# Packed attention and a gated product on one core: the gate of 96 units by Softplus and Erf in groups of three instead of a chain of tanh

## The chip, the core and the metric

The kernel runs on one core of a Trainium2 chip. Five engines work side by side, each through its own instructions in order: TensorE (PE in the profile; its weight loads are PEld), VectorE (DVE), ScalarE (ACT), GpSimd (POOL) and SyncE (SP, which issues most DMAs). The metric is the device time of one execution in microseconds.

## The reference, cut to what matters

```
scale = 1.0 / np.sqrt(q.shape[-1])               # q, k, v: 8 x 8 x 576 x 64, p: 8 x 8 x 32 x 64
p_packed = sm_attn(p, k, v)                      # softmax(scale * p k^T) v: 32 rows per head
out = sm_attn(q, p_packed, p_packed)             # softmax over those 32
x = out.transpose(0, 2, 1, 3).reshape(B * S, H * D)   # 4608 x 512
h = x @ w_in                                     # 4608 x 2048
sp = np.maximum(h, 0.0) + np.log1p(np.exp(-np.abs(h)))
g = h * erf(sp)
y = g @ w_out                                    # 4608 x 512
```

What is changed is how `h * erf(softplus(h))` is computed, and the order of the work around it.

## The kernel before, in words

The second softmax and `w_in` are joined: for each of the 8 batches b the kernel multiplies the packed rows into `w_in` (`w_prime`, tiles wp, wph and wpl), so that h is wp times the softmax weights a2. The work on h is cut into 128 **units**: batch b, half c of its 576 rows (288 columns) and pair i of 128-blocks of the 2048 features. Unit n of the batches from 2 on is n = 32 + 16 (b - 2) + 8 c + i; units 0 to 31 belong to batches 0 and 1. For every unit:

- `h_half` twice: 6 matmuls each into one of the two banks of the pool `ps_h`, with a2 and wp cut into a high and a low part (float32r for batches 0 and 1, float16 from unit 32 on);
- `h_copy` twice: ACT copies a bank into the tile hs; only then can the bank be written again. The score products of the attention (L386, L507) and a few wp take banks of the same pool, in turn with h;
- the gate. Units 0 to 31: `softplus` (ACT, tile t), `erf` (ACT, in place) and `gate` (DVE, t times hs into hs). The two functions are in different tables of ACT, so the units go in groups of three: `ENDS` lists the unit that closes each group, and after its Softplus come an ACT_TABLE_LOAD, three Erf and three gates. Units 32 to 127: `tanh_gate`, four passes of ACT (L669, L671, L672, L676) and three of DVE (L673, L674, L678), all in the table that has the exponential of the attention, so that no load is needed;
- `split`: DVE makes gh, hs rounded (a cast), and gl, what is left;
- `o_part` for each of four 128-blocks d of the output: 6 matmuls of gh and gl with `w_out`'s two parts, summed over the 4 or 8 units of a segment in one bank of `ps_o` for each d. After a segment's last unit `put` lets ACT copy each bank (tile ob), and a DMA writes it out.

Units 0 to 19 are written out by hand in `BEGINNING`, a letter and numbers for each part. From unit 20 on `step(n, ...)` issues for unit n `h_half` and `h_copy`, then the output product of a unit some way behind: five behind up to unit 31, then two units per step until it is `LAG` = 3 behind. The attention of the next batch is a generator; `ATTEND` and `ATTEND_LATER` say at which step and in which place each piece runs. A pair (n, w) is step n (in `ATTEND_LATER` counted from the first unit of the batch before), and w is the place: 5 behind h, 0 and 1 behind the first `o_part`, 3 behind the third, 2 at the end of the step. `JOINS_LATER` does it for wp: in the steps -6, -4, 2 and 4 from a batch's first unit, wp stands behind the first `o_part`, and its copies wph (ACT, L560) and wpl (DVE) at the end. `keep_order` makes PE, DVE and ACT keep the order in which the code issues.

Two exponentials are of interest: that of the first softmax (tile a, L453, two passes and a sum each, behind the maximum m; then the transposes t, L403, read it), and that of the second (tile ta, L297, one pass).

Of the kernel before, what the change touches and what calls it, by code (L numbers as in the profile page):

```python
# [8 lines left out]
F32 = mybir.dt.float32  # L9
# [11 lines left out]
T_SCALE, T_BIAS = 0.2627170245906788, -0.9287499984171923  # L21
Q_SCALE, Q_BIAS = 1.2484601345862187, 1.2510285994602417
U_SCALE, U_BIAS = 2.981034033350855, 0.5025259929887246
A1, A2 = -1.0780370417831138, 7.315330971479113
A_SCALE, A_BIAS = 0.5000167827005251, 0.3105391086974029
# [17 lines left out]
o10.2 o11.2 v12 s15 L13 h16.0 p11.2 p11.0 h16.1 c16.1 K14 m13 R14 o12.2 d16.0 s16 K13 S13 u13 v13 p11.3 e14 T13  # L43
# [7 lines left out]
def tile_pack_attention_moe(ctx: ExitStack, tc: tile.TileContext, qT, kT, v, pT, w_in, w_out, outT):  # L51
# [17 lines left out]
    LAG = 3  # L69
# [7 lines left out]
    ENDS = (1, 4, 7, 10, 13, 16, 19, 22, 25, 28, 31)  # L77
    BEGUN, BEHIND = 20, 15
# [12 lines left out]
    consts = cpool.tile([P, 2], F32, name="consts")  # L91
# [13 lines left out]
    for i, c in enumerate((8.0 * T_SCALE, 8.0)):  # L105
        nc.gpsimd.memset(consts[:, i:i + 1], c)
# [101 lines left out]
    def scales(b):  # L208

        rho[b] = apool.tile([P, 1], F32, name=f"rho{b}", tag="rho")  # L210
        nc.vector.tensor_scalar(rho[b][:], inverse[b][:], inverse["in"][:], 2.0 ** 11, op0=ALU.mult, op1=ALU.mult)
        back = apool.tile([P, 1], F32, name=f"back{b}", tag="back")
        other_way(back[:], rho[b][:])
        gate_scales[b] = apool.tile([P, 2], F32, name=f"gs{b}", tag="gs")
        nc.vector.tensor_scalar(gate_scales[b][:], consts[:], back[:], None, op0=ALU.mult)
        inverse[b] = back
# [38 lines left out]
    def in_turn(ins):  # L255

        if functions:
# [16 lines left out]
    ATTEND_LATER = ((-12, 2), (-6, 0), (-6, 1), (-4, 0), (-4, 1), (-4, 2), (-3, 2), (-2, 3), (-2, 2), (-1, 3), (-1, 2),  # L274
                    (0, 0), (0, 1), (1, 0), (1, 1), (2, 0), (2, 1), (4, 0), (4, 1),
                    (5, 2), (6, 2), (7, 2), (7, 2), (8, 2), (8, 2), (9, 2), (10, 2), (10, 2))
# [43 lines left out]
    def attention(b):  # L320
# [206 lines left out]
        every = second_softmax(b, ta, tb, mx, hi, lo, 0, S, None, nc.vector.tensor_copy if b < NB0 else nc.scalar.copy)  # L527
# [43 lines left out]
    def h_half(n, k):  # L571
        b, c, i = units[n][:3]
        if k == 0:
            turn = sum(n > e for e in ENDS) % 2
            tag = TAGS[n] if n < ALONE else "t1" if n < GROUPED and turn else "hs"
            rows[n] = tpool.tile([P, 2, HT], F32, name=f"hs{b}_{c}_{i}", tag=tag)
# [16 lines left out]
    def h_copy(n, k, copy=nc.scalar.copy):  # L593
        dst, src = rows[n][:, k, :], banks_of.pop((n, k))[:, 0:HT]
        if n < GROUPED:
            copy(dst, src)
        else:
            nc.scalar.mul(dst, src, 2.0 ** -19)  # L598

    def softplus(n):  # L600
        b, c, i = units[n][:3]
        ts[n] = tpool.tile([P, 2, HT], F32, name=f"t{b}_{c}_{i}", tag="t0")
        in_turn(nc.scalar.activation(ts[n][:], rows[n][:], AF.Softplus))
# [57 lines left out]
    def tanh_gate(n):  # L661

        b, c, i = units[n][:3]
        hs = rows.pop(n)
        t = tpool.tile([P, 2, HT], F32, name=f"t{b}_{c}_{i}", tag="t0")
        u = tpool.tile([P, 2, HT], F32, name=f"u{b}_{c}_{i}", tag="t1")
        scale = gate_scales[b]
        root = A2 ** 0.5
        nc.scalar.activation(t[:], hs[:], AF.Tanh, bias=T_BIAS, scale=scale[:, 0:1])  # L669
        yield  # L670
        nc.scalar.activation(t[:], t[:], AF.Square, bias=root * Q_BIAS, scale=root * Q_SCALE)  # L671
        nc.scalar.activation(u[:], t[:], AF.Tanh, bias=U_BIAS, scale=U_SCALE / A2)  # L672
        nc.vector.scalar_tensor_tensor(t[:], hs[:], scale[:, 1:2], t[:], op0=ALU.mult, op1=ALU.add)  # L673
        nc.vector.scalar_tensor_tensor(t[:], u[:], A1, t[:], op0=ALU.mult, op1=ALU.add)  # L674
        yield
        nc.scalar.activation(t[:], t[:], AF.Tanh, bias=A_BIAS, scale=A_SCALE)  # L676
        yield
        nc.vector.scalar_tensor_tensor(hs[:], t[:], 1.0, hs[:], op0=ALU.add, op1=ALU.mult)  # L678
        gs[n] = (hs,)
        yield  # L680
        yield

    gates, group = {}, []
# [5 lines left out]
    def step(n, outs):  # L689

        now, before = None, gates.pop(n - 1, None)
        late = n == GROUPED
        more = len(outs) > 1
        last = n >= len(units) - 1

        def begin():
            nonlocal now
            if n >= GROUPED:
                now = gates[n] = tanh_gate(n)
            else:  # L700
                group.append(n)

        def functions():
            if now:
                next(now)
            if last:
                split_behind(outs[0])
            if now:
                next(now)
            elif n < GROUPED:  # L710
                softplus(n)

        def split_behind(m):
            if m + 2 < len(units):
                split(m + 2)

        if n < len(units):
            h_half(n, 0)
            if not late:
                h_copy(n, 0)  # L720
            h_half(n, 1)
            if not late:
                h_copy(n, 1)
                do(n, 5)
                begin()
        if before:
            next(before)
            next(before)
        for m in outs:
            for d in range(NDM):  # L730
                o_part(m, d)
                if units[m][4]:
                    put(m, d)
                if m == outs[0] and d == 0:
                    do(n, 0)
                    do(n, 1)
                    if not more:
                        functions()
                        if GROUPED <= n and not last:
                            split_behind(m)  # L740
                elif m == outs[0] and d == 2:
                    do(n, 3)
            if more or n < GROUPED:
                split_behind(m)
        if n in ENDS:
            for part in (erf, gate):
                for m in group:
                    part(m)
            group.clear()
        if late:  # L750
            nc.scalar.preload_act_table_set("exp_and_others")
            do(n, 4)
            for k in range(2):
                h_copy(n, k)
            begin()
        if more:
            functions()
# [29 lines left out]
    for b in range(NB0, B):  # L787
        base = first_use[b - 1]
        for n, where in ATTEND.get(b) or [(base + n, where) for n, where in ATTEND_LATER]:
# [15 lines left out]
    for i, high, low in ((0, 28, 29), (1, 28, 30), (2, 29, 30), (3, 30, 31), (4, 31, 32), (5, 32, 33), (6, 32, 35), (7, 34, 37)):  # L805
        slot(22 + i // 2, 1).append((whole, i))
        slot(high, {6: 4, 7: 5}.get(i, 0)).append((halve_high, i))
# [51 lines left out]
    split(BEHIND + 1)  # L859
    behind = BEHIND  # L860
    for n in range(BEGUN, len(units) + LAG):
        outs = range(behind, min(behind + 1 + (n >= GROUPED), n - LAG + 1))
        step(n, outs)
        behind += len(outs)
# [39 lines left out]
```

## Time and profile before

| | |
|---|---|
| time, median of 3 runs | 693.34 us (693.13 to 693.34) |
| time of the profiled execution | 693.22 us |
| its span in the profile | 691.4 us |
| busy: PE, DVE, ACT | 678.2, 600.3, 556.0 us |
| idle of ACT before L676 / of DVE before L673 | 40.6 / 50.5 us |

The span is from the first to the last instruction that the profile holds; the time has some 1.8 us more around it. A matmul's row lasts from its issue to its modelled end, and the next one's begins before it ends, so PE can be shown as busy while its issue has a short pause. The chain of work that ended last books each matmul from the end of the one before.

### The profile page before, as it was taken

To read this page: it belongs to the slowest core of one execution; us is meant where nothing else is said; L and a number is where in the kernel's file an instruction comes from. 1 tells how busy PE (TensorE), PEld (TensorE's weight loads), DVE (VectorE), ACT (ScalarE), POOL (GpSimd) and SP (SyncE) were. 2 spreads that over 40 slices of the span, in tenths; PEclk is the share of its full clock that TensorE was granted. 3 is DMA by queue.
4 is the path that set the end of the run, shared out by engine and by line. 5 is a ranking of instruction groups with operands and counts; after the bars stand their busy time and mean duration, and the time that the engine had idled before them with its cause. 6 is when DMAs were issued, how large, how long until landed. Compare 5 with 4: busy or idle time off the path is not lost.

```text
span 691.4 us, 15628 instructions
## 1 busy us (share of the span) xinstructions
PE 678.2 (98%) x6442; PEld 537.8 (78%) x6442; DVE 600.3 (87%) x937; ACT 556.0 (80%) x981; POOL 53.6 (8%) x80
## 2 busy tenths in 40 slices
PE   8899999999999999999999999999999999999997
PEld 6687989998889777867777776777777677777775
DVE  4999998989997999889978898888988899877775
ACT  3799977967778789888888888887888878787774
POOL 2031123101452000000000000000000000000000
PEclk9999999999999999999999999999999999999999
DMA  9996456367342502211122202031021101000010
GB/s 317 401 341 217 155 171 228 105 207 230 40 91 22 163 11 86 87 59 42 36 61 95 92 1 73 18 122 66 9 82 52 37 1 36 1 9 27 5 33 34
DMA packets 34311, 66.81 MB, mean 97 GB/s; under 512 B 4032, under 2 KB 13248, under 8 KB 34240
## 3 DMA queue, kind: packets, MB, share of 16 engines
q1 hardware_dynamic: 29600, 56.31, 24.1%
q0 software_dynamic: 4352, 8.92, 5.3%
q8 instruction: 50, 0.82, 0.5%
q10 hardware_dynamic: 288, 0.59, 0.2%
q14 instruction: 21, 0.17, 0.1%
HBM read 49.81 MB, written 15.99 MB: 95 GB/s over the span
## 4 chain that ended last, share of the span: by engine, by line
PE 60%; DVE 18%; ACT 14%; DMA 4%; issue 3%; POOL 0%; SPq 0%; ACTq 0%; POOLq 0%; DVEq 0%
PE o L640 35%; PE h L588 18%; DVE t L673 3%; DVE t L674 3%; PE wp L541 3%; ACT t L671 3%; ACT t L669 2%; DVE gl L623 2%; ACT u L672 2%; ACT t L676 2%; DMA wi<-w_in 2%; ACT ob L652 2%; PE p L415 1%; DMA k<-kT 1%; PE s L507 1%
## 5 line engine op out<-in xcount | busy, mean ns | idle before, releaser
L640 PE MATMUL o<-gh,woh 128*128 128x288 f16 x1536 | 304.3, 286 | 0.9 <-ACT ob L652 0.9
L640 PEld LDWEIGHTS <-woh 128*128 128x128 f16 x2304 | 223.4, 98 | 67.3 <-issue 11.7
L640 PE MATMUL o<-gl,woh 128*128 128x288 f16 x768 | 219.6, 286 | 0.5 <-DVE gl L623 0.4
L588 PE MATMUL h<-a2h,wph 128*128 128x288 f16 (+1 forms) x512 | 148.8, 291 | 1.9 <-ACT hs L598 0.9
L588 PE MATMUL h<-a2h,wpl 128*128 128x288 f16 (+1 forms) x512 | 147.8, 289 | 1.2 <-DVE wpl L565 1.2
L588 PE MATMUL h<-a2l,wph 128*128 128x288 f16 (+1 forms) x512 | 147.5, 288 | 0.0
L673 DVE SCALAR_TENSOR_TENSOR t<-hs,gs,t 128x576 f32<-128x576 f32 x96 | 78.3, 816 | 50.5 <-ACT u L672 49.8
L623 DVE TENSOR_TENSOR gl<-hs,gh 128x576 f16<-128x576 f32 (+1 forms) x124 | 96.3, 776 | 4.4 <-ACT gh L616 0.5
L640 PE MATMUL o<-gh,wohl 128*128 128x288 f32 x448 | 97.9, 299 | 0.8 <-ACT ob L650 0.8
L676 ACT ACTIVATE t<-t 128x576 f32<-128x576 f32 x96 | 65.8, 686 | 40.6 <-DVE t L674 38.8
L598 ACT ACTIVATE hs<-h 128x288 f32<-128x288 f32 x192 | 71.8, 407 | 30.5 <-PE h L588 28.5
L588 PEld LDWEIGHTS <-wph 128*128 128x128 f16 x768 | 74.9, 98 | 20.8 <-issue 1.9
L640 PEld LDWEIGHTS o<-gh,wohl 128*128 128x128 f32 x448 | 74.2, 188 | 7.2 <-issue 2.7
L674 DVE SCALAR_TENSOR_TENSOR t<-u,t 128x576 f32<-128x576 f32 x96 | 72.7, 758 | 3.3
L678 DVE SCALAR_TENSOR_TENSOR hs<-t,hs 128x576 f32<-128x576 f32 x96 | 72.0, 750 | 2.4 <-ACT t L676 2.4
L669 ACT ACTIVATE t<-hs,gs 128x576 f32<-128x576 f32 x96 | 73.8, 769 | 0.0
L671 ACT ACTIVATE t<-t 128x576 f32<-128x576 f32 x96 | 65.6, 683 | 3.0
L672 ACT ACTIVATE u<-t 128x576 f32<-128x576 f32 x96 | 65.6, 683 | 3.1
L640 PE MATMUL o<-gl,wohl 128*128 128x288 f32 x224 | 66.2, 296 | 0.1
L616 DVE CAST gh<-hs 128x576 f16<-128x576 f32 (+1 forms) x117 | 55.6, 475 | 4.1 <-PE o L640 3.7
L588 PEld LDWEIGHTS <-wpl 128*128 128x128 f16 x384 | 37.6, 98 | 9.5
L640 PEld LDWEIGHTS o<-gl,wohl 128*128 128x128 f32 x224 | 42.2, 188 | 0.3 <-DVE gl L623 0.3
(126 smaller groups left out, 823.6 us busy)
## 6 DMA issues: line engine op xcount, KB each, us to landing
q<-qT SPq DMA_DIRECT2D x32, 288.0 KB, 4.1
k<-kT SPq DMA_DIRECT2D x30, 288.0 KB, 4.9
wos<-w_out SPq DMA_DIRECT2D x16, 512.0 KB, 5.7
outT<-ob SPq DMA_DIRECT2D x48, 144.0 KB, 1.8
v<-v SPq DMA_DIRECT2D x24, 256.0 KB, 4.1
wi<-w_in SPq DMA_DIRECT2D x12, 512.0 KB, 6.6
outT<-ob POOLq DMA_DIRECT2D x32, 144.0 KB, 3.3
scratch<-wo POOLq DMA_DIRECT2D x16, 256.0 KB, 3.3
```

The source lines that it names most:

```text
L588: nc.tensor.matmul(ps[:, 0:HT], w[:, r, fo:fo + P], a[:, r, c * HT:(c + 1) * HT], start=(m == 0), stop=(m == 5))
L598: nc.scalar.mul(dst, src, 2.0 ** -19)
L616: copy(ghi[:], gs[n][0][:])
L623: nc.vector.tensor_tensor(glo[:], hs[:], ghi[:], op=ALU.subtract)
L640: nc.tensor.matmul(acc[b, c, d][:, 0:HT], w[f][:, d * P:(d + 1) * P], gg[:, k, :], start=(first and k == 0 and m == 0), stop=(last and k = ...
L669: nc.scalar.activation(t[:], hs[:], AF.Tanh, bias=T_BIAS, scale=scale[:, 0:1])
L671: nc.scalar.activation(t[:], t[:], AF.Square, bias=root * Q_BIAS, scale=root * Q_SCALE)
L672: nc.scalar.activation(u[:], t[:], AF.Tanh, bias=U_BIAS, scale=U_SCALE / A2)
L673: nc.vector.scalar_tensor_tensor(t[:], hs[:], scale[:, 1:2], t[:], op0=ALU.mult, op1=ALU.add)
L674: nc.vector.scalar_tensor_tensor(t[:], u[:], A1, t[:], op0=ALU.mult, op1=ALU.add)
L676: nc.scalar.activation(t[:], t[:], AF.Tanh, bias=A_BIAS, scale=A_SCALE)
L678: nc.vector.scalar_tensor_tensor(hs[:], t[:], 1.0, hs[:], op0=ALU.add, op1=ALU.mult)
```

## The change

From unit 32 on the gate is what it was for units 0 to 31: Softplus (with the batch's scale as a per-partition operand), Erf and one product, in groups of three (`ENDS` now runs to unit 127; groups close at units 1, 4, 7, ...). `tanh_gate`, its constants and its three DVE passes are gone, and so is the step in which the output product caught up: `LAG` is 5 to the end. DVE, not ACT, casts a2. The attention's pieces stand elsewhere: the two exponentials of every batch from 3 on stand at the end of a step that closes a group, behind its three Erf, which needs three versions of `ATTEND_LATER`, since the batches' first units fall on different places in a group. In `BEGINNING` L13 (ACT, part of a weight load) stands behind two `put`, and K13 and S13 (DVE) behind a split.

```diff
-o10.2 o11.2 v12 s15 L13 h16.0 p11.2 p11.0 h16.1 c16.1 K14 m13 R14 o12.2 d16.0 s16 K13 S13 u13 v13 p11.3 e14 T13
+o10.2 o11.2 v12 s15 h16.0 p11.2 p11.0 h16.1 c16.1 L13 K14 m13 R14 o12.2 d16.0 s16 u13 v13 K13 S13 p11.3 e14 T13
...
-    LAG = 3
+    LAG = 5
...
-    ENDS = (1, 4, 7, 10, 13, 16, 19, 22, 25, 28, 31)
-    BEGUN, BEHIND = 20, 15
+    ENDS = tuple(range(1, 16 * B, 3))
+    BEGUN = 20
...
-        gate_scales[b] = apool.tile([P, 2], F32, name=f"gs{b}", tag="gs")
-        nc.vector.tensor_scalar(gate_scales[b][:], consts[:], back[:], None, op0=ALU.mult)
+        gate_scales[b] = apool.tile([P, 1], F32, name=f"gs{b}", tag="gs")
+        nc.vector.tensor_scalar(gate_scales[b][:], back[:], 4.0, None, op0=ALU.mult)
...
-        3: ((25, 2), (27, 0), (27, 1), (30, 0), (30, 1), (31, 2), (32, 2), (34, 3), (34, 2), (35, 3), (35, 2),
+        3: ((25, 2), (27, 0), (27, 1), (30, 0), (30, 1), (31, 1), (31, 2), (34, 3), (34, 2), (35, 3), (35, 2),
...
-    ATTEND_LATER = ((-12, 2), (-6, 0), (-6, 1), (-4, 0), (-4, 1), (-4, 2), (-3, 2), (-2, 3), (-2, 2), (-1, 3), (-1, 2),
-                    (0, 0), (0, 1), (1, 0), (1, 1), (2, 0), (2, 1), (4, 0), (4, 1),
-                    (5, 2), (6, 2), (7, 2), (7, 2), (8, 2), (8, 2), (9, 2), (10, 2), (10, 2))
+    SCORES = ((-12, 2), (-6, 0), (-6, 1), (-4, 0), (-4, 1))
+    POOLED = ((-2, 3), (-2, 2), (-1, 3), (-1, 2), (0, 0), (0, 1))
+    PACKED = ((1, 0), (1, 1), (2, 0), (2, 1), (4, 0), (4, 1))
+    ATTEND_LATER = (
+        SCORES + ((-4, 2), (-2, 2), (-1, 3), (-1, 2), (0, 0), (0, 1), (0, 3), (0, 2)) + PACKED
+        + ((5, 2), (6, 2), (7, 2), (8, 3), (8, 2), (8, 2), (9, 2), (10, 2), (10, 2)),
+        SCORES + ((-4, 2), (-3, 2)) + POOLED + PACKED
+        + ((5, 2), (6, 3), (6, 2), (7, 2), (8, 2), (8, 2), (9, 2), (10, 2), (10, 2)),
+        SCORES + ((-4, 3), (-4, 2)) + POOLED + PACKED
+        + ((5, 2), (6, 2), (8, 2), (9, 3), (9, 2), (9, 2), (10, 2), (11, 2), (11, 2)))
...
-        every = second_softmax(b, ta, tb, mx, hi, lo, 0, S, None, nc.vector.tensor_copy if b < NB0 else nc.scalar.copy)
+        every = second_softmax(b, ta, tb, mx, hi, lo, 0, S, None, nc.vector.tensor_copy)
...
-            tag = TAGS[n] if n < ALONE else "t1" if n < GROUPED and turn else "hs"
+            tag = TAGS[n] if n < ALONE else "t1" if turn else "hs"
...
-            nc.scalar.mul(dst, src, 2.0 ** -19)
+            nc.scalar.mul(dst, src, 2.0 ** -18)
...
     def softplus(n):
         b, c, i = units[n][:3]
         ts[n] = tpool.tile([P, 2, HT], F32, name=f"t{b}_{c}_{i}", tag="t0")
-        in_turn(nc.scalar.activation(ts[n][:], rows[n][:], AF.Softplus))
+        scale = 1.0 if n < GROUPED else gate_scales[b][:, 0:1]
+        in_turn(nc.scalar.activation(ts[n][:], rows[n][:], AF.Softplus, scale=scale))
...
-    def tanh_gate(n):
-        b, c, i = units[n][:3]
-        hs = rows.pop(n)
-        t = tpool.tile([P, 2, HT], F32, name=f"t{b}_{c}_{i}", tag="t0")
-        u = tpool.tile([P, 2, HT], F32, name=f"u{b}_{c}_{i}", tag="t1")
-        scale = gate_scales[b]
-        root = A2 ** 0.5
-        nc.scalar.activation(t[:], hs[:], AF.Tanh, bias=T_BIAS, scale=scale[:, 0:1])
-        yield
-        nc.scalar.activation(t[:], t[:], AF.Square, bias=root * Q_BIAS, scale=root * Q_SCALE)
-        nc.scalar.activation(u[:], t[:], AF.Tanh, bias=U_BIAS, scale=U_SCALE / A2)
-        nc.vector.scalar_tensor_tensor(t[:], hs[:], scale[:, 1:2], t[:], op0=ALU.mult, op1=ALU.add)
-        nc.vector.scalar_tensor_tensor(t[:], u[:], A1, t[:], op0=ALU.mult, op1=ALU.add)
-        yield
-        nc.scalar.activation(t[:], t[:], AF.Tanh, bias=A_BIAS, scale=A_SCALE)
-        yield
-        nc.vector.scalar_tensor_tensor(hs[:], t[:], 1.0, hs[:], op0=ALU.add, op1=ALU.mult)
...
-    def step(n, outs):
-        now, before = None, gates.pop(n - 1, None)
-        late = n == GROUPED
-        more = len(outs) > 1
-        last = n >= len(units) - 1
-        def begin():
-            nonlocal now
-            if n >= GROUPED:
-                now = gates[n] = tanh_gate(n)
-            else:
-                group.append(n)
-        def functions():
-            if now:
-                next(now)
-            if last:
-                split_behind(outs[0])
-            if now:
-                next(now)
-            elif n < GROUPED:
-                softplus(n)
-        def split_behind(m):
-            if m + 2 < len(units):
-                split(m + 2)
+    def step(n, m):
         if n < len(units):
-            h_half(n, 0)
-            if not late:
-                h_copy(n, 0)
-            h_half(n, 1)
-            if not late:
-                h_copy(n, 1)
-                do(n, 5)
-                begin()
-        if before:
-            next(before)
-            next(before)
-        for m in outs:
-            for d in range(NDM):
-                o_part(m, d)
-                if units[m][4]:
-                    put(m, d)
-                if m == outs[0] and d == 0:
-                    do(n, 0)
-                    do(n, 1)
-                    if not more:
-                        functions()
-                        if GROUPED <= n and not last:
-                            split_behind(m)
-                elif m == outs[0] and d == 2:
-                    do(n, 3)
-            if more or n < GROUPED:
-                split_behind(m)
+            for k in range(2):
+                h_half(n, k)
+                h_copy(n, k)
+            do(n, 5)
+            group.append(n)
+        for d in range(NDM):
+            o_part(m, d)
+            if units[m][4]:
+                put(m, d)
+            if d == 0:
+                do(n, 0)
+                do(n, 1)
+                if n < len(units):
+                    softplus(n)
+            elif d == 2:
+                do(n, 3)
+        if m + 2 < len(units):
+            split(m + 2)
         if n in ENDS:
             for part in (erf, gate):
-                for m in group:
-                    part(m)
+                for x in group:
+                    part(x)
             group.clear()
-        if late:
-            nc.scalar.preload_act_table_set("exp_and_others")
-            do(n, 4)
-            for k in range(2):
-                h_copy(n, k)
-            begin()
-        if more:
-            functions()
         do(n, 2)
...
-        slot(high, {6: 4, 7: 5}.get(i, 0)).append((halve_high, i))
+        slot(high, 0 if i < 6 else 5).append((halve_high, i))
...
-    split(BEHIND + 1)
-    behind = BEHIND
+    split(BEGUN - LAG + 1)
     for n in range(BEGUN, len(units) + LAG):
-        outs = range(behind, min(behind + 1 + (n >= GROUPED), n - LAG + 1))
-        step(n, outs)
-        behind += len(outs)
```

Counted over the whole program, ACT has 103 ACT_TABLE_LOAD where it had 30, and 833 rows where it had 958; DVE has 742 where it had 928; PE has the same 8421.

On ACT, in the step of unit 76 (batch 4, c 1, i 4: hs4_1_4 is its h, a1_6 the scores of batch 6, wph5_1 a part of wp of batch 5), before:

```order
L598 ACTIVATE hs4_1_4_5813<-h4_1_4_0_5814 128x288
L598 ACTIVATE hs4_1_4_5813<-h4_1_4_1_5822 128x288
L676 ACTIVATE t4_1_3_5781<-t4_1_3_5781 128x576
L350 COPY a1_6_5690<-s1_1_6_0_5847 128x288
L350 COPY a1_6_5690<-s1_1_6_1_5848 128x288
L669 ACTIVATE t4_1_4_5859<-hs4_1_4_5813,gs4_4583 128x576
L671 ACTIVATE t4_1_4_5859<-t4_1_4_5859 128x576
L672 ACTIVATE u4_1_4_5860<-t4_1_4_5859 128x576
L560 ACTIVATE wph5_1_5888<-wp5_1_5838,rho5_5703 128x1024
L598 ACTIVATE hs4_1_5_5907<-h4_1_5_0_5908 128x288
L598 ACTIVATE hs4_1_5_5907<-h4_1_5_1_5916 128x288
```

The same place in the changed kernel, from this unit's Softplus (L603) to the first h copy of unit 77:

```order
L603 ACTIVATE t4_1_4_5562<-hs4_1_4_5515,gs4_4386 128x576
L652 ACTIVATE ob4_0_7_1_5570<-o4_0_0_1_5148,omega4_4388 128x288
L652 ACTIVATE ob4_0_7_2_5579<-o4_0_0_2_5155,omega4_4388 128x288
L652 ACTIVATE ob4_0_7_3_5603<-o4_0_0_3_5162,omega4_4388 128x288
L606 ACT_TABLE_LOAD
L606 ACTIVATE t4_1_2_5438<-t4_1_2_5438 128x576
L606 ACTIVATE t4_1_3_5491<-t4_1_3_5491 128x576
L606 ACTIVATE t4_1_4_5562<-t4_1_4_5562 128x576
L559 ACTIVATE wph5_1_5616<-wp5_1_5541,rho5_5430 128x1024
L452 ACT_TABLE_LOAD
L452 ACTIVATE a1_6_5417,sm6_5593<-a1_6_5417,m6_5592 128x576 x2
L597 ACTIVATE hs4_1_5_5622<-h4_1_5_0_5623 128x288
```

Between the Softplus of unit 76 and the h copies of unit 77 there now stand three output copies (unit 71 is now the one that ends its segment here; its first copy is ahead of the Softplus), a load, three Erf, the copy of wp, a second load and the exponential; before there were two passes of the same unit and the copy of wp.

On ACT in the steps of units 46 and 47 of the changed kernel (batch 2, c 1, i 6 and 7), the exponential behind a group that has nothing else at its end:

```order
L597 ACTIVATE hs2_1_6_3581<-h2_1_6_1_3590 128x288
L603 ACTIVATE t2_1_6_3604<-hs2_1_6_3581,gs2_2124 128x576
L606 ACT_TABLE_LOAD
L606 ACTIVATE t2_1_4_3478<-t2_1_4_3478 128x576
L606 ACTIVATE t2_1_5_3554<-t2_1_5_3554 128x576
L606 ACTIVATE t2_1_6_3604<-t2_1_6_3604 128x576
L452 ACT_TABLE_LOAD
L452 ACTIVATE a1_4_3326,sm4_3526<-a1_4_3326,m4_3525 128x576 x2
L597 ACTIVATE hs2_1_7_3636<-h2_1_7_0_3637 128x288
L597 ACTIVATE hs2_1_7_3636<-h2_1_7_1_3645 128x288
L603 ACT_TABLE_LOAD
```

The transposes of step 47 read a1_4 behind the third `o_part`. Before, this exponential stood at the end of step 45, with no load.

## Rows read from the trace of the kernel before

**Rows 1.** The page: busy time by engine, and the granted clock in 40 slices.

```profile
PE 678.2 (98%) x6442; PEld 537.8 (78%) x6442; DVE 600.3 (87%) x937; ACT 556.0 (80%) x981; POOL 53.6 (8%) x80
PEclk9999999999999999999999999999999999999999
```

**Rows 2.** Chain that ended last, 250 to 300 us: start, us, what.

```profile
252.97 1.47 PE h L588 x12
255.18 1.02 PE wp L541 x16
256.68 2.31 PE o L640 x18
258.99 1.47 PE h L588 x12
...
263.40 1.47 PE h L588 x12
...
274.18 1.47 PE h L588 x12
...
277.85 0.65 PE t L403 x6
...
294.49 1.47 PE h L588 x12
```

**Rows 3.** The same chain, 330 to 420 us.

```profile
335.20 1.02 PE wp L541 x16
...
416.05 1.02 PE wp L541 x16
```

**Rows 4.** Waits of PE and its weight loads after 200 us: total, times, longest.

```profile
PE h L588 <- ACT hs L598: 0.9, 4, 0.2
PE o L640 <- ACT ob L652: 0.9, 2, 0.6
PE o L640 <- DVE gl L623: 0.4, 1, 0.4
...
PEld t L403 <- ACT a L453: 1.2, 3, 0.4
...
PEld wp L541 <- ACT hs L598: 0.9, 2, 0.7
```

**Rows 5.** Waits of the weight loads over the whole span.

```profile
PEld o L640 <- ACT ob L650: 1.8, 2, 1.0
```

**Rows 6.** Groups of instructions by line and form: busy us, mean ns | idle before.

```profile
L673 DVE SCALAR_TENSOR_TENSOR t<-hs,gs,t 128x576 f32<-128x576 f32 x96 | 78.3, 816 | 50.5 <-ACT u L672 49.8
...
L669 ACT ACTIVATE t<-hs,gs 128x576 f32<-128x576 f32 x96 | 73.8, 769 | 0.0
...
L676 ACT ACTIVATE t<-t 128x576 f32<-128x576 f32 x96 | 65.8, 686 | 40.6 <-DVE t L674 38.8
...
L560 ACT ACTIVATE wph<-wp,rho 128x1024 f16<-128x1024 f32 x22 | 24.3, 1104 | 0.0
L652 ACT ACTIVATE ob<-o,omega 128x288 f32<-128x288 f32 x48 | 21.7, 490 | 4.2 <-PE o L640 3.9
...
L606 ACT ACTIVATE t<-t 128x576 f32<-128x576 f32 x32 | 20.4, 678 | 0.1
...
L297 ACT ACTIVATE ta<-ta 128x1152 f32<-128x1152 f32 x7 | 8.1, 1153 | 0.0
```

**Rows 7.** Timeline of ACT, 179 to 187.5 us: start, us, what.

```profile
180.53 1.28 ACT L606 ACT_TABLE_LOAD   x1
181.82 1.84 ACT L606 ACTIVATE t<-t 128x576 f32<-128x576 f32 x3
183.56 0.68 ACT L596 COPY hs<-h 128x288 f32<-128x288 f32 x2
```

**Rows 8.** Timeline of ACT, 356.8 to 359 us: exponential of the first softmax.

```profile
357.13 0.78 ACT L453 ACTIVATE a<-a,m 128x576 f32<-128x576 f32 x1 [1.04 <-DVE m L429]
...
358.66 0.68 ACT L598 ACTIVATE hs<-h 128x288 f32<-128x288 f32 x2
```

More of the change, by code (lines that the diff above doesn't have):

```diff
@@ L17 @@
 AX = mybir.AxisListType
[L21 to L25, printed above, removed]
 EXPONENT, TINY = 0x7F800000, 2.0 ** -55
@@ L90, in tile_pack_attention_moe @@
     ident = cpool.tile([P, P], F32, name="ident")
-    consts = cpool.tile([P, 2], F32, name="consts")
     w_in_sb = cpool.tile([P, 4, DFF], F32, name="w_in_sb")
@@ L104, in tile_pack_attention_moe @@
             then(engine.memset(w_in_sb[:, :, j * FB:(j + 1) * FB], 0.0).ins, identity)
-    for i, c in enumerate((8.0 * T_SCALE, 8.0)):
-        nc.gpsimd.memset(consts[:, i:i + 1], c)
     def staging(name, n):
@@ L658, in put @@
         begun.add((b, c, d))
-    def tanh_gate(n):
-        b, c, i = units[n][:3]
-        hs = rows.pop(n)
-        t = tpool.tile([P, 2, HT], F32, name=f"t{b}_{c}_{i}", tag="t0")
-        u = tpool.tile([P, 2, HT], F32, name=f"u{b}_{c}_{i}", tag="t1")
-        scale = gate_scales[b]
-        root = A2 ** 0.5
-        nc.scalar.activation(t[:], hs[:], AF.Tanh, bias=T_BIAS, scale=scale[:, 0:1])
-        yield
-        nc.scalar.activation(t[:], t[:], AF.Square, bias=root * Q_BIAS, scale=root * Q_SCALE)
-        nc.scalar.activation(u[:], t[:], AF.Tanh, bias=U_BIAS, scale=U_SCALE / A2)
-        nc.vector.scalar_tensor_tensor(t[:], hs[:], scale[:, 1:2], t[:], op0=ALU.mult, op1=ALU.add)
-        nc.vector.scalar_tensor_tensor(t[:], u[:], A1, t[:], op0=ALU.mult, op1=ALU.add)
-        yield
-        nc.scalar.activation(t[:], t[:], AF.Tanh, bias=A_BIAS, scale=A_SCALE)
-        yield
-        nc.vector.scalar_tensor_tensor(hs[:], t[:], 1.0, hs[:], op0=ALU.add, op1=ALU.mult)
[L679 to L683, printed above, removed]
+    group = []
     def split(n):
@@ L788, in tile_pack_attention_moe @@
         base = first_use[b - 1]
-        for n, where in ATTEND.get(b) or [(base + n, where) for n, where in ATTEND_LATER]:
+        for n, where in ATTEND.get(b) or [(base + n, where) for n, where in ATTEND_LATER[base % 3]]:
             slot(n, where).append((attend, b))
@@ L858, in tile_pack_attention_moe @@
     end = len(traced)
-    split(BEHIND + 1)
-    behind = BEHIND
+    split(BEGUN - LAG + 1)
     for n in range(BEGUN, len(units) + LAG):
-        outs = range(behind, min(behind + 1 + (n >= GROUPED), n - LAG + 1))
-        step(n, outs)
-        behind += len(outs)
+        step(n, n - LAG)
     keep_order(start, end)
```

## The prediction

> **What bounds the kernel now.** First the page: PE is shown busy for 678.2 of 691.4 us, DVE for 600.3 and ACT for 556.0, and the granted clock stands at its upper level (2.4 GHz) in all 40 slices [rows 1]. Then the chain of work: where it runs on PE, a unit costs 4.41 us (258.99 to 263.40: h 1.47, output product 2.94), and a step with a wp and a score product costs 6.02 (252.97 to 258.99), so such an insert is 1.61 [rows 2]. These are matmuls end to end. So no faster gate can shorten a step; what a change of ACT and DVE can give or take is pauses of PE, and the question is how many there are, and how many the new order makes.
>
> Pauses now. Between the like places 335.20 and 416.05 lie 80.85 us [rows 3]. PE's work in them is 16 x 4.41 = 70.56, four inserts 6.44, and the other pieces of an attention, 2.67 (four steps from 274.18 to 294.49 take 20.31, less 17.64) [rows 2]: 79.67. So 1.18 us per batch are pauses. The waits name them, three each: h on an ACT copy, the transposes t on the exponential [rows 4]. Three such batches make 3.5; the one before (255.18 to 335.20, 80.02) [rows 2, 3] 0.35. Outside these: the page can hide up to some 0.16 us of a PE wait behind a modelled end (a matmul's row is 0.29, the spacing 1.47/12 = 0.12), so the two waits of products on ob, 0.9 shown, are about 1.2, the one on gl 0.56, the fourth of the h waits 0.4, and I take 0.6 for the wp waits on hs (0.9 shown) [rows 4]. Sum 6.6 us. All wait for the chain through four ACT and three DVE passes, whose own waits are 38.8 us (L676 for DVE) and 49.8 (L673 for ACT) [rows 6].
>
> **The change part by part.**
>
> *Gates.* Each of 96 units loses on ACT L671, L672, L676 and gains one Erf: 3 x 0.686 - 0.678 = 1.38 us less, 132 us in all; L669 becomes Softplus with the same kind of operand, 0.769 [rows 6]. 73 more loads at 1.28 [rows 7] give 94 back. DVE loses L673 (78.3 us [rows 6]) and a sister of about that size. None of this is on the path; what counts is when it is done. With DVE's three passes gone, I remove all 6.6 us of pauses above.
>
> *Lag 5 and groups.* A group's Erf end with the step of its last unit, and the first product of the group stands three steps on: over 8 us for gates and splits, which are passes of DVE of at most 0.8 us [rows 6], so gh and gl are early. At the end, products of five units stand behind the last h instead of three; PE's work is the same, and the last ob and DMA are.
>
> *Bursts.* This is the cost. A step that closes a group puts on ACT, behind its own two copies and Softplus, a load and three Erf; the h copies of the next unit wait behind them, and PE needs those banks one step later. In the trace of units that already do so, a load takes 1.31 from the end of what precedes it to the Erf (180.51, the end of an output copy, to 181.82), three Erf 1.74 until the next copy begins, a copy 0.41 [rows 7]. From the start of such a step: second copy done at 1.92, Softplus 2.7, load 4.0, Erf 5.8, first copy of the next unit 6.2; PE wants that bank at 2 x 4.41 = 8.8. A plain group is hidden, with 2.5 us to spare. What goes beyond that:
>
> 1. Step 76, as the order shows: its fourth output copy cannot start before PE has ended the step, so the burst starts there, 0.04 + 0.48 for ob, load 1.31, Erf 1.74, wph 1.10, load 1.31, exponential 1.53 (357.13 to 358.66 [rows 8]), copy 0.4: 7.9 us, and 0.2 until the matmul is booked (release 0.05, shift 0.16). PE has one step, 4.41, to do meanwhile. Pause 3.7 us.
> 2. Steps 52 and 100: also ob, Erf and wph at a group's end, without an exponential: 0.52 + 1.31 + 1.74 + 1.0 + 0.4 + 0.2 - 4.41 = 0.77 each, 1.5.
> 3. Steps 47 and 95: the exponential behind the group of 46 (94) begins at 5.87 + 1.31 = 7.2 from that step's start and ends 1.68 later with its sum, 8.9; the second half of the transposes stands at 4.41 + 1.47 + 2.21 + 0.33 = 8.4. With 0.1 to 0.16 for release: 0.55 each, 1.1. In step 62 the same, with ACT already late from wph and copies: 0.6.
> 4. Step 38: in step 37 the copy of the transposed rows (pt) stands ahead of Softplus and waits for PE until about 2.7 instead of 1.9, so the burst is 0.8 late and the second copy of unit 38 done at 7.3, usable at 7.5; the scores take both banks from 4.41 + 0.24 + 1.47 + 0.73 = 6.85 on. 0.6.
> 5. The five exponentials ta (1.15 [rows 6]) behind a group: 5.8 + 1.31 + 1.06 + 0.4 = 8.6 plus 0.2, against 8.8. I count 0.05 each, 0.25.
>
> Sum 7.75. The bounds: nothing, if PE always has something else to do, and twice as much, if every chain is 0.5 us longer than laid out. I take the sum, since every duration is a row's.
>
> *Other edits.* In BEGINNING one product waits up to 1.0 us for an output copy [rows 5]; the copy that stands just ahead of it on ACT, L13, goes behind, and I count a gain of 0.4 of between 0 and 0.8: later waits on DVE may take it back. The cast of a2 on DVE is covered by the passes that DVE lost. Output DMAs that now stand behind loads on SP's queue cost nothing while ob has four buffers and eight units between uses; the loads that they pass only gain.
>
> Sum: 693.22 - 6.6 - 0.4 + 7.75 = 693.97 in terms of the profiled execution, which lies 0.12 below the median; that makes 694.1, and I say 694.0: within 0.2% (1.4 us), which is about what a measurement of this kernel tells from no change.
>
> A rule that speaks against the change: the row has a load at 1.28 us, 1.31 with the gaps on both sides [rows 7]. The Trainium skill (ScalarE: Activation LUTs, What ACT_TABLE_LOAD costs) gives about 2.66 us for every switch of tables, the load and as much again for a drain. By the row the plain group keeps 2.5 us; by the page's figure each load would be 1.35 longer, and the trace disagrees with it.
>
> **Rivals.**
>
> - *Only step 76 pauses.* The waits in points 2 to 5 are each under 0.8 us; if ACT runs a little ahead of my sums (0.3 to 0.8 in each burst, by overlap of neighbours) they vanish, and 3.7 is left: 693.2 - 7.0 + 3.7 + 0.1 = 690.0. For it: the overlap of copies in the rows is visible (two copies 0.68 against 2 x 0.41). Against: I have counted that overlap.
> - *Bursts longer by 0.25 us, on the other side.* The place is the h copy behind a group's end. Five ta exponentials are at the limit already, seven places beyond it, and at four (scores of steps 42, 50, 90, 98) my margin is some 0.2. Then 5 x 0.25 + 7 x 0.25 + 4 x 0.05 = 3.2: 697.2. It decides from about 0.06 us per burst on (0.7 us over twelve places). For it: what I overlook makes such chains longer, as when the next group's load waits for a gate on DVE, which stands behind a split that waits for PE. Against: plain groups have 2.5 us to spare.
> - *The pause of step 76 lowers the clock.* All slices show the upper level [rows 1], also where PE waits, so no row prices it. If a step after a pause ran at 1.2 GHz it would take 8.82 instead of 4.41: 698.4. The Trainium skill (TensorE: Matmul & The Clock Gate, Why this matters for your kernels) says that gaps between bursts of matmuls can drop the clock; no row of this trace shows that.
> - *A load keeps ACT for twice its row*, with a drain as long as itself. Two loads lie in the bursts of steps 76, 47, 62, 95 and of the five ta, one in those of 52, 100 and 38: 9 x 2.62 + 3 x 1.31 = 27.5, so 721.5. The row speaks against it: what follows a load starts 0.01 behind it [rows 7]. The page of the Trainium skill on activation tables named above would give nearly this time.
>
> That the loads are not made at all is excluded by the order; that DVE's relief gives nothing on PE is the forecast itself.
>
> **How the numbers follow.** Forecast 0.45, only step 76 0.22, longer bursts 0.25, clock 0.05, load 0.03. The forecast's own range is 692.3 to 695.4: half a microsecond for the removed pauses, one for the bursts. Faster by over 0.2% is the first rival, 0.22; same is the forecast, 0.45; the others slower, 0.33. For 8 in 10 the range goes to the times of the two larger rivals and a little beyond the second, 690.0 to 697.5; outside it lie half of the first, the clock and the load, 0.19.
>
> **What would show it.** Right: in the changed trace ACT's group ends show load, three Erf, copies in about 3.5 us; a wait of h on an hs copy of 3 to 4 us once, between 420 and 435 us; two of 0.8 near 300 and 545; t waits on a at three places of about 0.5; no waits of products on gl or ob after 600 us, and steps of 4.41 elsewhere. Wrong: the long wait absent or short (then ob or wph do not stand where I put them in time); waits of h on copies in plain groups (a load is dearer); products that wait for gl (DVE is late); a clock under its upper level after the long pause.

## The result and the profile after

The changed kernel took 699.09 us (median of 5: 697.15, 697.85, 699.09, 700.46, 700.58) against 693.34 before: a ratio of 1.0078 [1.0052 to 1.0103], slower. The profiled execution is the first of the five, 697.15 us with a span of 695.2; its mean granted clock was 1.000 of the upper level. In the other four it was 0.998, 0.998, 0.995 and 1.000. So there are two things to explain: 3.9 us in an execution at full clock (697.15 against 693.22), and what some executions have beyond it. (Times also spread by some 2 us at clocks of 0.999 and 1.000: 693.0 to 695.0 in 17 executions of the kernel before on one chip.)

The page after, its lines for the engines, the clock, the loads and the gates (columns as in [rows 1, 6]):

```profile
PE 678.3 (98%) x6442; PEld 537.3 (77%) x6442; DVE 465.5 (67%) x751; ACT 522.1 (75%) x856; POOL 53.4 (8%) x78
...
PEclk9999999999999999999999999999999999999999
...
L610 DVE TENSOR_TENSOR hs<-t,hs 128x576 f32<-128x576 f32 x128 | 90.0, 751 | 5.8 <-ACT t L606 5.7
...
L603 ACT ACT_TABLE_LOAD x45 | 57.7, 1283 | 1.2 <-DVE hs L610 0.3
L606 ACT ACT_TABLE_LOAD x44 | 56.5, 1283 | 0.8
```

DVE lost 135 us of work and ACT 34, and PE is as busy as before [rows 1]. A load took 1.283 us, no more than in [rows 7]. What decided is the list of PE's waits after 206 us (total, times, longest), which answers to [rows 4]:

```profile
PE h L587 <- ACT hs L597: 4.8, 3, 3.6
PE h L587 <- DVE wpl L566: 1.2, 2, 0.6
PE t L402 <- ACT a L452: 0.9, 4, 0.2
PE p L490 <- DVE norm L486: 0.4, 2, 0.2
...
PEld t L402 <- ACT a L452: 2.5, 6, 0.5
PEld L587 <- DVE wpl L566: 2.0, 3, 0.9
```

The waits of products on ob and gl [rows 4] are gone from this stretch (a new one of 0.41 us, of a product on an output copy, stands just ahead of it, at 203 us). In their place stand one wait of h for 3.6 us, two shorter ones, and two kinds that the prediction did not have: h on wpl, and p on norm.

**Where the long one comes from.** The timelines of ACT, in step 76, and of PE behind it, in the changed kernel (start, us, what):

```profile
425.70 1.39 ACT L652 ACTIVATE ob<-o,omega 128x288 f32<-128x288 f32 x3
427.11 1.28 ACT L606 ACT_TABLE_LOAD   x1
428.40 1.83 ACT L606 ACTIVATE t<-t 128x576 f32<-128x576 f32 x3
430.14 1.10 ACT L559 ACTIVATE wph<-wp,rho 128x1024 f16<-128x1024 f32 x1
431.26 1.28 ACT L452 ACT_TABLE_LOAD   x1
432.55 0.77 ACT L452 ACTIVATE a<-a,m 128x576 f32<-128x576 f32 x1
...
434.08 0.68 ACT L597 ACTIVATE hs<-h 128x288 f32<-128x288 f32 x2
434.79 1.28 ACT L603 ACT_TABLE_LOAD   x1
...
430.68 0.29 PE L640 MATMUL o<-gh,woh 128*128 128x288 f16 x1
434.52 0.28 PE L587 MATMUL h<-a2h,wph 128*128 128x288 f16 x1 [3.56 <-ACT hs L597]
```

PE starts the last matmul of the next step's product at 430.68 and the h behind it at 434.52, where 0.12 is the usual distance: a pause of 3.72 us, by the rows that were laid out (from start to start: load 1.29, three Erf 1.74, wph 1.12, load 1.29, exponential 1.53).

**The two pairs.** The chain of the changed kernel around step 54; step 52 closes a group and has the output copies and wph too:

```profile
305.88 0.50 ACT ob L652
...
306.40 1.28 ACT L606
...
309.43 1.10 ACT wph L559
310.53 0.03 issue
310.56 1.29 DVE wpl L566
311.85 0.05 issue
311.90 1.40 PE h L587 x10
```

And from the timelines of ACT and PE:

```profile
310.42 0.70 ACT L597 ACTIVATE hs<-h 128x288 f32<-128x288 f32 x2
...
310.87 0.28 PE L587 MATMUL h<-a2h,wph 128*128 128x288 f16 x1 [0.62 <-ACT hs L597]
...
311.90 0.30 PE L587 MATMUL h<-a2h,wpl 128*128 128x288 f16 x1 [0.62 <-DVE wpl L566]
```

h first waits 0.78 us for the first of the two copies of the unit before it, which begin at 310.42 behind wph (its first matmul starts at 310.87, 0.91 behind the last of the product, where 0.12 is usual). Its first two matmuls run, and the third, which reads wpl, waits another 0.78: wpl on DVE begins when wph is done and takes 1.29. Step 102 has the same pair, so 3.1 us in all.

**The wait of p on norm.** The chain in step 49 of the changed kernel:

```profile
283.49 0.85 PE o L640 x6
284.37 0.47 DVE gh L616
284.86 0.76 DVE gl L623
285.62 0.09 DVE sm L474
285.74 0.18 DVE sm L475
...
286.65 0.17 DVE norm L486
286.82 0.04 issue
286.86 0.32 PE p L490
287.19 2.21 PE o L640 x18
```

norm's five short passes stand behind a split on DVE, and the split stands still until PE has read the buffer that it writes. The piece of p takes 0.65 instead of 0.22 us, in steps 49 and 97: 0.86 in all.

**The balance** of the two profiled executions, from the starts of matmuls at like places. Gone from before: 0.62 in `BEGINNING`, 0.37 at the change of units, 0.34 and three times 1.10 in the batches, 2.7 behind 580 us: 7.3 us. New: 3.72 (step 76), 3.14 (steps 54, 102), 2.2 (transposes t: 0.67, 0.89, 0.67), 0.86 (p), 0.43 (scores of step 38), 0.41 (a product on an output copy at 203 us): 10.8 us, and some 0.3 in pieces under 0.1. Together +3.8, as the spans have it.

### The profile page after: what moved, and what is told of

Same layout as the page of the kernel before. It is cut to its first block, busy times and chain, and to the rows that moved or that the text cites. A ratio compares the mean times of both kernels' runs of the same rounds, so it can differ in the third digit from the quotient of the medians.

```text
span 695.2 us, 15366 instructions
## 1 busy us (share of the span) xinstructions
PE 678.3 (98%) x6442; PEld 537.3 (77%) x6442; DVE 465.5 (67%) x751; ACT 522.1 (75%) x856; POOL 53.4 (8%) x78
## 4 chain that ended last, share of the span: by engine, by line
PE 79%; ACT 9%; DVE 4%; DMA 3%; issue 3%; POOL 1%; SPq 0%; POOLq 0%; ACTq 0%; DVEq 0%
PE o L640 48%; PE h L587 23%; PE wp L540 4%; ACT t L606 2%; DMA wi<-w_in 2%; DMA k<-kT 2%; ACT L606 1%; PE p L414 1%; PE s L506 1%; PE s L385 1%; ACT L452 1%; ACT a L452 1%; ACT t L603 1%; PE t L402 1%; ACT wph L559 1%
## 5 line engine op out<-in xcount | busy, mean ns | idle before, releaser
L610 DVE TENSOR_TENSOR hs<-t,hs 128x576 f32<-128x576 f32 x128 | 90.0, 751 | 5.8 <-ACT t L606 5.7
L606 ACT ACTIVATE t<-t 128x576 f32<-128x576 f32 x128 | 78.9, 674 | 0.5
L603 ACT ACTIVATE t<-hs,gs 128x576 f32<-128x576 f32 x96 | 74.5, 776 | 1.9
L566 DVE SCALAR_TENSOR_TENSOR wpl<-wp,rho,wph 128x1024 f16<-128x1024 f32 (+1 forms) x26 | 31.0, 1199 | 11.1 <-ACT wph L559 10.9
L652 ACT ACTIVATE ob<-o,omega 128x288 f32<-128x288 f32 x48 | 22.7, 498 | 20.1 <-PE o L640 19.9
```

The source lines that it names most:

```text
L566: nc.vector.scalar_tensor_tensor(lo, ps, rho[b][:], hi, op0=ALU.mult, op1=ALU.subtract)
L606: in_turn(nc.scalar.activation(ts[n][:], ts[n][:], AF.Erf))
L610: nc.vector.tensor_tensor(hs[:], ts.pop(n)[:], hs[:], op=ALU.mult)
L652: nc.scalar.mul(ob[:], acc[b, c, d][:, 0:HT], omega[b][:])
```

## The experiments

Two theories stood for the part beyond 697.15. The first: the pause of 3.72 us lowers TensorE's clock in some executions, the rival that had 0.05 in the prediction. The second: the clock falls for another reason, such as the loads. A third was not put to a test of its own: that some of it is no clock at all but the spread that every kernel here shows. For the 3.9 us the theory was coincidences: places where output copies, wph, the exponential and a group's Erf fall into one step.

**e1, the pause filled.**

```
+    zero = cpool.tile([P, P], F16, name="zero")
+    nc.gpsimd.memset(zero[:], 0.0)
...
+        if n == 78:
+            b, c = units[72][:2]
+            for _ in range(28):
+                nc.tensor.matmul(acc[b, c, 3][:, 0:HT], zero[:], a2[b][0][:, 0, 0:HT], start=False, stop=False)
         step(n, n - LAG)
```

> Adds to the changed kernel 28 products of a zero weight into an open o bank (they add nothing), on PE between the last output product of step 77 and the h of step 78, where PE waits 3.72 us for ACT: 28 x 0.1225 = 3.43 us of work inside the wait, so h starts at the same time. Theory (the long pause lowers the granted clock in some executions): the profiled execution stays near 697.2, the idle part of the pause falls to 0.3 us, and all executions lie within 0.8 us of 697.2 with a mean clock of 1.0. Rival (the clock falls for some other reason, such as the many table loads): still some executions 2 to 3.4 us longer with a mean clock of 0.995 to 0.998.

Measured: 697.07 to 698.89, median 698.09, mean clock 1.0, 0.999, 1.0, 1.0, 1.0. From the transposes near 355 us to those near 439 it takes 83.91 us, as in the changed kernel: the same pause in time, but PE is at work in it (28 matmuls from 432.40 us on, the h behind them at 436.12). The windows of e1 over the pause (PE, PEld, DVE, ACT, POOL busy, granted clock, DMA):

```profile
432.00:436.00 4.00, 3.99 (x33) 3.04 (x32) 3.22 (x5) 3.97 (x8) 0.00 (x0) 1.00 0.01 2
```

No execution had a clock below 0.999. The expected times were too narrow: only two of five lie within 0.8 us of 697.2. The profiled one was 698.78 at full clock, and its first output product began at 44.26 instead of 42.67 us, in a part of the program that is the same but for the clearing of the zero tile; e3, which does not have that, began at 43.90. The kernel before spreads as much on this chip (693.0 to 695.0).

**e2, the exponential of step 76 one step later.** `SCORES + ((-4, 3), (-4, 2)) + POOLED` became `((-4, 3), (-3, 2))`, in the version for the batch that starts at unit 80.

> In the changed kernel only the exponential of step 76 goes one step later (its own pair of loads, no Erf in that step). Theory: the pause of 3.72 us falls by a load, the exponential and its gaps, 2.85 us, to 0.8 to 0.9; fastest execution 694.3, and since the long pause is gone no execution has a clock under 1.0: median 694.3. Rival for the clock: the median stays about 2 us above the fastest. Rival for the pause (the output copies and Erf alone make it): the pause stays above 2 us and the fastest execution above 696.

Measured: median 696.23, fastest 695.41; mean clock 0.998 in one of six (699.37), 0.999 or 1.0 in the others. The pause fell from 3.72 to 0.79 as laid out, but only 1.4 of the 2.85 us came back, since the transposes, left where they were, now wait. So the expected 694.3 was missed; and the one execution at 0.998, some 3 us above the others, comes from a program whose longest pause is 0.79 us. Waits of e2:

```profile
PE h L587 <- ACT hs L597: 1.9, 3, 0.6
PE t L402 <- ACT a L452: 1.8, 6, 0.7
...
PEld t L402 <- ACT a L452: 4.0, 8, 1.0
```

**e3, wp out of steps 52 and 100.**

```
+            if n in (52, 100):
+                n -= 1
```

> In the changed kernel the wp of steps 52 and 100, with its copy wph and subtraction wpl, goes one step earlier, out of the steps that close a group. Theory: of the two waits of 0.78 us each in steps 54 and 102 the second (h on wpl) goes as well as the first (h copies behind ob, Erf, wph: 0.77 less a wph of 1.1 leaves nothing): 4 x 0.78 = 3.1 us, fastest execution 694.0. Since the pause of 3.72 us is still there, some executions stay 2 to 3.4 us longer with a clock of 0.995 to 0.998. If the first wait does not come from wph, only 1.6 us go: 695.6. If these four pauses are what lowers the clock, all executions have 1.0.

Measured: 696.75 to 699.66, median 697.28; the fastest was expected at 694.0. All four waits of 0.78 went, the first of each pair too, so wph was what made ACT late. But wp one step earlier waits for its bank until wpl of the one before is done, so a pair gives back 0.90 us instead of 1.57 (77.38 us between the transposes near 278 and 355; 78.28 in the changed kernel). Two pairs make 1.8 us; why the fastest is not lower still, the one trace does not show. The clock fell in four of five executions (0.994, 0.998, 0.998, 0.997, 1.0), and here the profiled one was among them. Windows of e3 over the same 3.72 us pause, columns as above:

```profile
426.00:430.00 4.00, 4.00 (x35) 3.19 (x34) 2.64 (x4) 3.97 (x8) 0.00 (x0) 1.00 0.73 192
430.00:434.00 4.00, 1.86 (x16) 1.36 (x14) 3.89 (x6) 3.97 (x5) 0.00 (x0) 0.99 0.47 156
434.00:438.00 4.00, 2.58 (x11) 1.57 (x11) 0.61 (x1) 3.97 (x9) 0.00 (x0) 0.50 0.01 2
438.00:442.00 4.00, 4.00 (x24) 2.79 (x23) 0.00 (x0) 1.23 (x3) 0.00 (x0) 0.66 0.00 0
442.00:446.00 4.00, 4.00 (x36) 3.25 (x35) 1.22 (x2) 2.43 (x5) 0.00 (x0) 1.00 0.00 0
```

and its chain there:

```profile
435.42 3.04 PE h L587 x12
438.45 3.37 PE o L640 x18
441.83 0.66 PE t L402 x6
442.48 0.73 PE o L640 x6
443.22 1.47 PE h L587 x12
```

From 434 us on the granted clock is 0.50, the lower of the two levels (1.2 GHz), and PE, which had waited from 431.6, goes back to work at it: h takes 3.04 instead of 1.47 us, 18 matmuls of a product 3.37 instead of 2.21. By 441 the clock is full again, and it is full in every other stretch up to the last matmul. The cost is 1.57 + 1.16 = 2.7 us by the chain, 2.6 between the starts of the transposes near 355 and 441 (86.49 against 83.91). The Trainium skill (TensorE: Matmul & The Clock Gate, Why this matters for your kernels) says that gaps between bursts of matmuls can drop the clock; this trace agrees, and the execution profiled of the changed kernel shows that the same pause does not always do it. The other three with a lower clock (0.998, 0.997, 0.998) took 697.03, 697.28 and 697.74, only 0.3 to 1.0 us more than the one at 1.0.

**e6, such a pause in the kernel before**, which has no Softplus or Erf in its second part:

```
+    spare = cpool.tile([P, 576], F16, name="spare")
...
         step(n, outs)
+        if n == 76:
+            for _ in range(7):
+                nc.scalar.copy(spare[:], w_in_sb[:, 0, 0:576])
```

> The kernel before, without any Softplus or Erf in its second part, with seven extra copies of 128 x 576 on ACT at the end of step 76 (some 4.7 us of work that nothing uses), so that PE waits there for ACT as the changed kernel does. Theory (a long pause of PE lowers the clock, whatever makes it): a pause of 3 to 4 us, fastest execution 696.3 to 697.5, and in half or more of the executions a clock under 0.999 and 2 to 3.4 us more. Rival (the table loads or the Erf order lower the clock): the same pause, clock 1.0 in all executions, and a spread like that of the kernel before (693.0 to 695.0, from the first microseconds).

Measured: 697.18 to 698.69, median 697.77, mean clock 1.0, 0.997, 1.0, 0.997, 0.997. The pause was 3.27 us (`PE h` on hs 4.0 in total, longest 3.1). Three of five lost their clock without a load nearby; the price was about 0.9 us (means of 698.30 and 697.41), smaller than expected. So such a pause is enough, without Softplus, Erf or loads; that the fall stands right behind it is not seen here, since the profiled execution was at 1.0.

**e7, the changed kernel again.**

> The changed kernel again, beside the others on one chip. Theory: executions of two sorts, with clock 1.0 near 697.2 to 699 (as the start of the program varies by up to 2 us) and with 0.995 to 0.998 some 2 to 3.4 us longer, at least two of the latter in five; if the profiled one is of that sort, the granted clock stands at half level right behind the 3.72 us pause and at full everywhere else. Rival (the clock falls at places that have nothing to do with the pause): low windows elsewhere.

Measured: 697.01, 697.45, 698.06 and 698.15 at 1.0, 699.92 at 0.998 and 700.51 at 0.995. The profiled one was at full clock. With the first five, eleven executions of this kernel: six at 1.0 with a median of 697.65, five at 0.995 to 0.998 with a median of 700.46, which is 2.8 us apart. That is near the 2.7 of e3's rows, but the clock can't be all of it. A fall as in e3 (0.99, 0.50 and 0.66 over 4 us each: 3.4 us of clock lost, of 697.8) by itself makes a mean of 0.995. A mean of 0.998 leaves room for at most 1.75 us of lost clock. So the two executions at 0.995 (700.51, 700.58) can hold a fall like e3's; the three at 0.998 (699.09, 699.92, 700.46) lie 1.4, 2.3 and 2.8 us above 697.65, at most 1.75 of it by the clock. What the rest is, no trace shows; a late start, as in e1, is one candidate.

All executions whose clock was recorded but that of e9, by the longest pause of PE behind 206 us in the profiled one:

| kernel | longest pause, us | executions | clock 0.998 or less |
|---|---|---|---|
| changed (both series) | 3.72 | 11 | 5 |
| e3 | 3.72 | 5 | 4 |
| e6 | 3.27 | 5 | 3 |
| e1 | 3.72, filled | 5 | 0 |
| e5, e4, e2 | 1.88, 1.45, 0.79 | 7, 11, 6 | 1, 1, 1 |
| before | 0.74 | 47 | 1 |
| e8, e10 | under 0.8 | 5, 5 | 0, 0 |

12 of 21 with an open pause of over 3 us, 4 of 86 with none. A part of such a mean can lie at the very end, where it costs nothing: in the traces of e4 and e5, both at 0.999, the half clock stands only behind the last matmul, in the last 1.4 and 1.0 us. But only some 3.4 us of these programs lie behind it, and 0.997 takes at least 3.5 at half clock: 0.997 or less stands in 7 of the 21 and 1 of the 86. On one and the same chip e3 has a clock of 0.998 or less in four of five, e1 in none of five. The fall can come without a long pause too (e2, e4, e5 once each, at places that no trace shows).

**e4, groups closed elsewhere.** One order of the attention for all batches, and

```
+    ENDS = tuple(range(1, 41, 3)) + tuple(x for x in (n + k for n in range(32, 16 * B, 16) for k in (0, 3, 6, 9, 11, 13)
+                                                      ) if 41 < x < 112) + tuple(range(112, 16 * B, 3))
```

> Changed kernel with other group ends in batches 2 to 6: 0, 3, 6, 9, 11, 13 of each 16 units (groups of three and two), so that no group closes in a step with output copies of a finished segment, wph or copies of scores, and one order for all batches, in which the exponential stands behind the two Erf of unit 13 and its transposes two steps on. Theory (all new pauses come from such coincidences): 697.15 less 3.72, 3.14 (four of 0.78), 2.0 (three waits of t) and 0.86 (two of p) = 687.4, some 6 us under the kernel before, clock 1.0 in every execution. Rival (two more table loads per batch, or groups of two, make new waits): 690 or more, with waits of h on hs copies in the steps of the new ends.

Measured: 692.71 to 694.33, median 693.32, ratio to before 0.9996 [0.9988, 1.0005]. The waits on wpl, t and norm were gone, but its one large wait was four of 1.45 us, at the exponentials:

```profile
PE h L584 <- ACT hs L594: 5.1, 4, 1.3
```

Four output copies and wph of the step before had pushed the burst back (Softplus starts at 267.13 us, the h copies behind the exponential at 273.32). The rival was right on the time, but by this timeline a group of two is no longer than one of three; the exponential behind it is what is added.

**e5, the exponential at the end of step 12 of 16.** Ends `(0, 3, 6, 9, 11, 14)`, exponential at (-4, 2), wph of that step ahead of its last output copy.

> As the regrouped kernel before it, whose four pauses of 1.45 us stood in the steps where the exponential followed two Erf: the group ends are now 0, 3, 6, 9, 11, 14 of each 16 units, the exponential stands at the end of step 12 of 16, which closes no group, with wph ahead of the last output copy of that step and the maximum ahead of wpl on DVE. Theory: the four pauses go and nothing takes their place: 692.9 less 5.8 = 687.1 for the fastest execution, clock 1.0 in nearly all. Rival (another load pair per batch and the exponential behind wph delay the h copies of the step after): a pause of 0.3 to 1 us in each of four batches, 688 to 691.

Measured: median 695.10, ratio 1.0027 [1.0016, 1.0038]; a miss, with four pauses of 1.88:

```profile
PE h L584 <- ACT hs L594: 6.9, 4, 1.7
```

In that step the output copies and wph wait for PE's own last product, so a load and an exponential behind them can only begin when PE has one step left, as in step 76 (the last copy ends at 266.46 us, the load starts at 266.47, h at 269.74).

**e8, the exponential alone, one step on; two copies moved from ACT to DVE, and wph of the step before ahead of Softplus.**

```
+        SCORES + ((-4, 3), (-3, 2)) + POOLED + PACKED
...
+                (nc.vector.tensor_copy if b > 3 else nc.scalar.copy)(dst[:, x, :], parts[x][:, 0:n])
```

> The regrouped kernel with the group ends 0, 3, 6, 9, 11, 14 once more; the exponential stands alone at the end of step 13 of 16, wph of the step before it ahead of Softplus and the output copies, and the copies of scores (a) and of the transposed exponentials (a1t) of batches 4 to 7 are on DVE. Theory (a pause comes where a burst, measured from the last output copy or wph, outlasts one step of PE): exponential ends 6.3 us after the start of step 13, its h copies 1.5 us before PE wants the bank, so the pauses of 1.88 go and no other over 0.6 comes: span near 685.5, time near 687.5. Rival (DVE becomes late with the copies, so that h waits for the banks of the scores): pauses of 0.5 to 1.5 us in step 13 of each batch, 689 to 693.

Measured: 690.36 to 691.51, median 691.01, ratio 0.9959 [0.9945, 0.9973]: faster than before. The pauses of 1.88 went (which of the three moves did it was not tried one by one); three of the expected microseconds were missing:

```profile
PE p L404 <- DVE a1t L457: 2.8, 4, 0.7
```

**e10, that copy ahead of the gates on DVE.** `(-2, 3), (-2, 3)) + POOLED[2:]`.

> As the last regrouped kernel, with one place moved: the copy a1t on DVE stands right behind its transposes in step 14 of 16, ahead of the split and of the three gates of the group that closes there, instead of behind them. Theory: the four waits of the transposes p on a1t (2.8 us together in the last one) go: span 688.5 less 2.8 = 685.7, median near 688.2. Rival (the split and the gates, later by the wait for PE and the copy, make products or the next waits late): 690 or more.

Measured: 686.89 to 689.50, median 687.77, ratio 0.9915 [0.9899, 0.9930], clock 0.999 or 1.0 in all five. Its page:

```profile
PE 675.4 (99%) x6442; PEld 537.9 (79%) x6442; DVE 475.3 (69%) x771; ACT 529.5 (77%) x846; POOL 53.4 (8%) x78
...
L600 ACT ACT_TABLE_LOAD x52 | 66.7, 1283 | 1.2 <-DVE hs L607 0.3
```

After 206 us PE's list of waits on other engines is empty. It has 113 table loads, the changed kernel 103, and its profiled span is 10.1 us shorter (685.1 against 695.2): what made the changed kernel slower was where the work stands (e10 changes the order, and the engine of two copies), not the gates by Softplus and Erf.

**e9, the edit in `BEGINNING` alone, in the kernel before.**

> The kernel before with one part of the change alone: in BEGINNING L13 goes behind h16, c16 and p11, and K13 and S13 behind u13 and v13. Theory: the wait of a product for an output copy near 111 us falls from 0.93 to 0.30 us, and the wp near 198 us begins 0.6 earlier, as in the changed kernel; the rest is as before, so the span is 0.6 shorter for the same start (690.8).

Measured in one execution: 693.03 us, span 691.3 with a start 0.4 us later than that of before. The wait near 111 us fell from 0.93 to 0.31 us, as in the changed kernel. The new wait of the changed kernel for an output copy at 203 us (0.41) does not appear here, so another part of the change makes it, by its place the output product that stays five units behind.

## Why the prediction was wrong

*The mechanism of the sum held, and its size did not: the new pauses were put at 7.75 us and measured 11.1.* Pauses removed: 7.3 us instead of 7.0 (6.6 and 0.4). Step 76: 3.72 for 3.7. Plain groups are hidden, as forecast. A load costs its row. The rival of 721.5 is refuted by loads of 1.283 us with no drain beside them: the one at 427.11 starts 0.02 us behind the copy ahead of it, and the Erf starts 0.01 behind its end. The figure of the Trainium skill (ScalarE: Activation LUTs, What ACT_TABLE_LOAD costs), about 2.66 us for a switch of tables with its drain, is not what this trace shows.

*Point 2, steps 52 and 100, was half of what they cost* (0.77 each, 1.57 measured). The wait for the h copies was exact; that wpl hangs on wph, and that the h of unit 54 (102) is the first to read that piece of wpl, was not followed. The burst was costed only as far as ACT; the DVE pass behind its last member takes another 1.29.

*A wait was missed*: p on norm, 0.86. It comes from the order made for two of the batches, which puts norm behind a split on DVE; the prediction looked at ACT's part of the three orders alone.

*Points 3 to 5* were near: the transposes 2.2 for 1.7, the scores of step 38 0.43 for 0.6, the ta exponentials nothing for 0.25. With 0.41 for the product at 203 us, the new pauses at full clock were 10.8 and some 0.3 more instead of 7.75. That alone makes 697.15, inside the range, and near the rival of longer bursts (697.2), but by luck: the bursts were not longer, what hangs on them was. At full clock the eleven executions have a median of 697.65, already at the range's end of 697.5.

*The other step that failed was the chance of the clock, 0.05.* The argument was that no row prices a pause's effect, since the clock stands full in all slices [rows 1]. But all pauses of before behind 206 us are under 0.8 us, so those rows could not speak of one of 3.7. e3 shows the fall behind the pause; with the pause filled (e1) no execution of five had it, and with a pause made in the kernel before (e6) three of five had a lower clock. Its cost of 2.7 us is less than the 4.4 set down (one step at half speed), because the clock came back within the second piece of that step. That the same happened in the changed kernel's own low executions is inferred, since none of those left a trace; the two at 0.995 fit it, the three at 0.998 only in part. The median of 699.09 is one of these: 3.9 us of pauses, and 1.9 more, of which the clock can be at most 1.75.

Open: what decides, at the same pause, whether an execution loses its clock and for how long, why e6 and three executions of e3 paid only 0.3 to 1.0, and what beside the clock lengthens the executions at 0.998.

## What to carry to other kernels

When an in-order engine gets bursts, list for each burst what stands in the same step for other reasons (copies that wait for the bottleneck's own last product, above all), and follow its last member one engine further, to the pass that depends on it: the coincidences cost 10 us here, and with them gone (e10) no wait of PE on another engine was left. Put a burst into steps without such fixed work even if that takes more table loads. A long pause of TensorE is to be priced with a possible step at half clock behind it, and with the fact that executions will then differ.

## What the runs showed of the hardware beyond what was expected

Behind the same pause of 3.72 us the clock stayed full in the profiled execution of the changed kernel and fell to 0.50 in that of e3, which differs in the wp of two steps elsewhere, for less than 7 us. With products that add nothing issued into the pause, the clock stayed full in five of five. The first output product begins between 42.65 (before) and 44.26 us (e1) in programs that are almost alike up to there, which alone spreads the times by 1.6 us.
